# Local attention and two expert layers on one core: keys copied per lead tile, one score product per head, half the products on zeros, a fourth decode buffer

## Chip, core and metric

The kernel runs on one core of one Trainium2 chip. The metric is the device time of one execution in microseconds (us). A core has five engines that run their own instruction lists in order and wait for one another through semaphores: TensorE (PE in the profile, with its weight loads as PEld), VectorE (DVE), ScalarE (ACT), GpSimd (POOL) and SyncE (SP, which here issues the transfers).

## The reference

Inputs are q, k, v of 2 batches, 8 heads, 768 positions and 64 elements a head, and two pairs of weights. All arithmetic is float32.

```
scores_l = q @ k.T / 8           only where |pos_q - pos_k| < 16, else -1e9
scores_s = q @ max of k over blocks of 32 / 8 + log(32)
a = softmax over [scores_l, scores_s];  x = a @ [v, mean of v over blocks of 32]
x = (1536 tokens, 512);  h = relu(x @ w_in);  x = (h*h) @ w_out        2048 wide
h = x @ w_in2;  out = (h * sigmoid(h)) @ w_out2                         2048 wide
```

## The kernel before

Attention is worked out in 24 tiles of 64 queries. A tile of a batch needs 96 keys around its queries and the 24 block summaries, so 120 columns of scores (`NK`) for each head. Two heads lie side by side on the 128 partitions (a head pair, hp 0 to 3), so a head pair is two products of 64 rows that run together. The expert layers take the 1536 tokens in three blocks of 512, and each layer's 2048 hidden columns in 16 chunks of 128. A chunk s is `gemm1(s)` (tile `h`, 12 products of 512 columns), relu, square and a split into a high and a low part (`gh`, `gl`, tile `g`), then `gemm2(s)` (tile `acc`, 12 products). Every weight chunk (`wi`, `wo`) arrives as raw 64-bit numbers and is decoded: `sc` on ScalarE, `sh`, `st1`, `st2` on VectorE, `hi` on ScalarE, `lo` on VectorE. The product of `sc` lies in tile `c`, of which there are `NSPL` = 3. For `wo` chunks `c` is also written out to memory (`scr`), and the tile is free only when that transfer has landed.

The first eight tiles are the **lead**: no expert product can start before all eight are through, since the first block of 512 tokens is exactly these eight. They are loaded in bulk: `t_ksum` (all keys of batch 0, one tile for each head pair), `qrlead` (queries, two halves of four tiles), `vrows` (values for the block means), `vlead` (values, two halves). For each lead tile and head pair `psl` forms the scores on TensorE, `ttl` (line 397) adds the mask and takes the maximum on VectorE, `exl` (line 402) is the exponential on ScalarE. For each tile follow `ze`, `rc`, `nt` (the norm, VectorE), `psa` (four transposes, TensorE), `a` (a copy on ScalarE), `av` (16 short products), and `xh`, `xl` (high and low half of x, on ScalarE and VectorE). Block means of the values come from six products `vs` into tile `psv`, which ScalarE copies out in two wide copies `vmean` (24x2048 into `vlead`) ahead of the first `av`. `av` of the lead goes to one of four PSUM banks (tag `acc`), so the fifth waits for the `xl` of the first.

`psl` before takes two pairs of products for a head pair: one with 96 columns straight from a window of `t_ksum`, one with 24 columns from `ksum`. Ahead of all this TensorE runs `WARM` = 20 products on a tile of zeros (`idle_in`, `idle_out`).

The order of the first block, lead and 16 chunks with the attention of tiles 8 to 15 between them, is not written by hand: `first_order()` is a planner with a duration, a due time and dependencies for every step. It gives a fixed list, and each engine's instructions stand in the order of that list, SyncE's transfers too. After the first block a scheduler places the remaining attention tiles among the products of the second block.

Of the kernel before, what the change touches and what calls it, by code (L numbers as in the profile page):

```python
# [10 lines left out]
F32 = mybir.dt.float32  # L11
# [25 lines left out]
LAG = 2  # L37
NSPL = 3
NWO = 6
# [8 lines left out]
NGRP = 4  # L48
WARM = 20
NEG = -1.0e9  # L50
# [3 lines left out]
def first_order():  # L54
# [13 lines left out]
    def tile_due(g):  # L68
        return .25 * g if g < NLEAD else 46 + 11 * (g - NLEAD)

    def chunk_due(s):
        return 30 + 7 * s

# [5 lines left out]
    for hp in range(NHP):  # L79
        op("vec", "ksum", hp, 1.0, -50 + hp, [("kt", hp, 0)])  # L80
    for c in range(6):
        op("pe", "vs", c, .92, 1.7 + .1 * c, [("vr", c // 2, 0)])
    for i in range(NLEAD // NGRP):
# [4 lines left out]
    for j in range(4 * NHP):  # L88
        due = tile_due(TPB) - 28 + j
        load("kv", j, 196, due - 4, [("kvr", j - 2, A)] * (j >= 2))  # L90
        op("vec", "kvr", j, .52, due, [("kv", j, 0)])
# [3 lines left out]
    for g in range(NFIRST):  # L95
        due, two = tile_due(g), g - 2 >= NLEAD
        if g < NLEAD:
            for hp in range(NHP):
                op("pe", "psl", (g, hp), .38, due, [("kt", hp, 0), ("ksum", hp, A), ("q", g // NGRP, 0)] +
                   [("psl", (g, hp - 1), 0)] * (hp > 0), bank=None if hp else ("acc", "ttl", (g, NHP - 1)))  # L100
                op("vec", "ttl", (g, hp), .21, due, [("psl", (g, hp), M), ("cst", 0, 0)])
                op("act", "exl", (g, hp), .385, due, [("ttl", (g, hp), A)])
            exp = [("exl", (g, hp), A) for hp in range(NHP)]
        else:
            load("kw", g, 246, due - 9, [("pss", g - 2, M)] * two)
            load("qr", g, 131, due - 8.9, [("side", g - 2, A)] * two)
            load("vf", g, 196, due - 6, [("av", g - 2, M)] * two)
            op("pool", "side", g, 1.2, due, [("qr", g, 0)] + [("pss", g - 2, M)] * two)
            op("vec", "kwc", g, .13, due - .5, [("kw", g, 0)] + [("kvr", 4 * NHP - 1, 0)] * (g >= TPB))
            if TPB <= g < TPB + NVF:  # L110
                op("vec", "vfc", g, .35, due, [("vf", g, 0), ("vendc", 0, A)])
            op("pe", "pss", g, 1.1, due, [("kwc", g, A), ("side", g, A)] + [("gemm1", 1, 0)] * (g == NLEAD), bank=("att", "ttr", g))
            op("vec", "ttr", g, .84, due, [("pss", g, M), ("psa", g - 2, M)])
            op("act", "exp", g, 1.54, due, [("ttr", g, -.45)])
            exp = [("exp", g, A)]
# [4 lines left out]
        else:  # L120
            op("act", "nt", g, 1.2, due, [("rc", g, A)])
        op("pe", "psa", g, .62, due, [("nt", g, -.1)], bank=("att", "a", g))
        op("act", "a", g, .56, due, [("psa", g, M)] + [("av", g - 2, M)] * two)
        values = [("vl", g // NGRP, 0), ("vmean", g // NGRP, A)] if g < NLEAD else [("vf", g, 0), ("vfm", g % NVF, A)]
# [6 lines left out]
    for i, (x, s) in enumerate(chunks):  # L131
        due = chunk_due(s) - 11 + .5 * (x == "wo") - 20 * (not i)
        load("raw", (x, s), 524, chunk_due(s) - 14 + .5 * (x == "wo") - 100 * (not i),
# [23 lines left out]

    free = dict.fromkeys(("sp", "act", "vec", "pe", "pool"), 0.0)
    end, banks, moved = {}, dict(att=[], acc=[]), 2.0
# [15 lines left out]
    while todo:  # L175
# [5 lines left out]
        t, _, _, o = min(picks)  # L181
        t, _, _, o = min((p for p in picks if p[3]["eng"] == o["eng"] and p[0] <= t + .1), key=lambda p: p[1:3])
        todo.remove(o)
# [12 lines left out]
def kernel(  # L196
# [126 lines left out]
    def again_wo(kept, m, name):  # L323
# [18 lines left out]
    qd = [cp.tile([P, NHP, QT], F32, tag=f"qd{i}", name=f"qd{i}") for i in range(NQD)]  # L342
    qrlead = [first_p.tile([P, NGRP, QT * NHP], F32, tag="qr", name="qrlead0"),
              wi_p.tile([P, NGRP, QT * NHP], F32, tag="wi", name="qrlead1")]
    vlead = first_p.tile([P, NLEAD, H, D], F32, tag="vf", name="vlead")
# [95 lines left out]
    def a_copy(g):  # L441
        d = st[g]
        a = d.pop("pa")[0:NK].rearrange("p c q -> p (c q)")
        if g >= NLEAD:
            d["a"] = p2.tile([P, 512], F32, tag="a", name=f"a{g}")
        copy(act, d["a"][0:NK], a)
# [126 lines left out]
    def first_block():  # L573
# [8 lines left out]
        for _ in range(WARM):  # L582
            mm(idle_out, idle_in[:, 0:P], idle_in, start=True, stop=True)
        for g in range(NLEAD):

# [31 lines left out]


        def psl(ghp):
            g, hp = ghp  # L620
            if hp == 0:
                st[g]["ps"] = ps_acc.tile([P, NHP, NK], F32, tag="acc", name=f"pss{g}")
            q = qrlead[g // NGRP][:, g % NGRP].rearrange("p (q c) -> p c q", c=NHP)
            for keys, to in ((kts[hp][:, g * QT:g * QT + NWIN], slice(0, NWIN)), (ksum[0][:, hp], slice(NWIN, NK))):
                for e in range(2):
                    pr = slice(64 * e, 64 * e + 64)
                    mm(st[g]["ps"][pr, hp, to], q[pr, hp], keys[pr], start=True, stop=True)

# [86 lines left out]
        def xh(g):  # L715
            if g * QT >= BLOCKS[0]:
                leave_lead()
            x_high(g)

        do = dict(kt=kt, q=q, cst=cst_, vr=vr, vl=vl, ksum=ksum_, vs=vs, vmean=vmean, vfm=vfm, kv=kv, kvr=kvr,  # L720
                  vend=vend, vendc=vendc, vfc=vfc, kw=kw_load, qr=q_load, vf=v_load, side=side_by_side, kwc=k_sums,
# [174 lines left out]
```

## Time and profile before

| | us |
|---|---|
| median of 3 runs | 620.21 |
| lowest, highest | 617.1, 620.78 |
| the profiled execution, its own time | 621.01 |
| its span, first to last instruction | 619.2 |
| TensorE busy | 606.7 (98%) |
| VectorE busy | 340.3 (55%) |
| ScalarE busy | 301.3 (49%) |

The profile is of one execution. A time of 1.81 us lies around its span. Busy shares are means over stages that differ: up to about 46 us the lead runs, up to about 163 us the first block, and from there almost only products. The view by stretches tells these apart. Matmuls are pipelined, and their durations overlap, so that a busy TensorE is not one at its peak; the distance between starts says more than a product's duration.

### The profile page before, as it was taken

The page shows a single profiled execution, that of the slowest core. Times are in us where ns is not written, and L with a number is a line of the kernel's source. Part 1 is how long each engine was busy: PE and PEld are TensorE (multiplying, and loading weights), DVE is VectorE, ACT ScalarE, POOL GpSimd, SP SyncE. Part 2 cuts the span into 40 slices and gives each one's busy share as a digit, 9 for nine tenths or more (in the row PEclk, how much of TensorE's full clock was granted, in tenths as well). Part 3 has the DMA queues.
Part 4 walks back from the last instruction along what each step waited for, and adds up shares of the span by engine and source line. Part 5 has one row for each costly group of instructions (what it writes and reads, how often), then busy time and mean ns, then how long its engine had stood idle before and what let it go on. Part 6 is the DMA issues. An engine that isn't in the chain of part 4 may idle for free.

```text
span 619.2 us, 9053 instructions
## 1 busy us (share of the span) xinstructions
PE 606.7 (98%) x3332; PEld 491.2 (79%) x3332; DVE 340.3 (55%) x785; ACT 301.3 (49%) x665; POOL 52.2 (8%) x61
## 2 busy tenths in 40 slices
PE   9979999899999999999999999999999999999997
PEld 7758786677888877888888888888888888888886
DVE  4899989994455544375555687665322222322222
ACT  3779978697544544365555554443212221222221
POOL 0011000101443443100000000000000000000000
PEclk9989999999999999999999999999999999999999
DMA  9977888665355455446564334515500233400211
GB/s 302 298 209 265 260 273 279 218 208 170 133 178 198 156 178 204 153 171 214 191 202 133 105 103 169 200 73 203 169 1 2 68 103 102 137 0 1 102 35 68
DMA packets 36619, 96.51 MB, mean 156 GB/s; under 512 B 3936, under 2 KB 11232, under 8 KB 36576
## 3 DMA queue, kind: packets, MB, share of 16 engines
q1 hardware_dynamic: 36576, 95.95, 47.0%
q8 instruction: 26, 0.43, 0.3%
q14 instruction: 17, 0.14, 0.1%
HBM read 74.96 MB, written 20.97 MB: 155 GB/s over the span
## 4 chain that ended last, share of the span: by engine, by line
PE 82%; DVE 10%; DMA 4%; ACT 3%; issue 1%; DVEq 0%; ACTq 0%
PE acc L229 37%; PE h L229 37%; PE pss L229 4%; DMA t_kv<-in_kT_dram 2%; PE av L229 2%; PE idle_out L229 1%; DVE c_wo L289 1%; DMA scr_dram<-c_wo 1%; PE psa L439 1%; DVE raw_wi L285 1%; DVE c_wi L289 1%; DVE wi L237 1%; DVE raw_wo L285 1%; DVE wo L237 1%; DMA t_kv<-in_vT_dram 1%
## 5 line engine op out<-in xcount | busy, mean ns | idle before, releaser
L229 PE MATMUL h<-xt,wi 128*128 128x512 f32 x576 | 142.4, 395 | 0.0
L229 PE MATMUL acc<-g,wo 128*128 128x512 f32 x576 | 140.2, 392 | 0.2 <-DVE g L237 0.2
L229 PE MATMUL h<-xt,wj 128*128 128x512 f32 x576 | 139.0, 391 | 0.0
L229 PEld LDWEIGHTS h<-xt,wj 128*128 128x128 f32 x576 | 108.1, 188 | 23.5 <-DVE r L237 0.2
L229 PEld LDWEIGHTS acc<-g,wo 128*128 128x128 f32 x576 | 107.5, 188 | 23.5 <-issue 0.6
L229 PEld LDWEIGHTS h<-xt,wi 128*128 128x128 f32 x576 | 106.5, 188 | 23.0 <-issue 1.0
L237 DVE TENSOR_TENSOR g<-r,g 128x512 fp32r<-128x512 f32 x96 | 80.5, 838 | 74.3 <-ACT g L233 38.4
L237 DVE TENSOR_TENSOR r<-h,r 128x512 f32<-128x512 f32 x48 | 33.2, 691 | 114.2 <-ACT r L535 113.7
L535 ACT ACTIVATE r<-h 128x512 f32<-128x512 f32 x48 | 28.7, 597 | 117.5 <-PE h L229 117.4
L233 ACT ACTIVATE g<-r 128x512 fp32r<-128x512 f32 x80 | 50.5, 631 | 35.3 <-DVE r L237 34.5
L229 PE MATMUL acc<-wq,g 128*128 128x512 f32 x240 | 57.3, 390 | 0.0
L229 PE MATMUL acc<-wo,g 128*128 128x512 f32 x216 | 53.6, 397 | 0.0
L229 PEld LDWEIGHTS acc<-wq,g 128*128 128x128 f32 x240 | 45.1, 188 | 9.3
L402 ACT ACTIVATE T<-T,m 128x120 f32<-128x120 f32 x96 | 36.8, 385 | 27.5 <-DVE m L397 27.2
L229 PEld LDWEIGHTS acc<-wo,g 128*128 128x128 f32 x216 | 40.7, 188 | 9.7
L229 PE MATMUL acc<-wp,g 128*128 128x512 f32 x120 | 28.8, 390 | 0.0
L233 ACT ACTIVATE wo<-c_wo 128x512 fp32r<-128x512 f32 x38 | 23.7, 622 | 7.8 <-DVE c_wo L289 7.6
L527 ACT ACTIVATE r<-h 128x512 f32<-128x512 f32 x16 | 9.6, 598 | 34.6 <-PE h L229 34.6
L229 PEld LDWEIGHTS acc<-wp,g 128*128 128x128 f32 x120 | 22.5, 188 | 4.7
L234 POOL COPY qd<-qr 128x256 f32<-128x256 f32 x16 | 14.9, 930 | 133.3 <-PE pss L229 85.3
L397 DVE CUSTOM_DVE_ANT_0 T<-pss,cst_sb 128x120 f32<-128x120 f32 x96 | 21.9, 276 | 7.3 <-PE pss L229 7.3
L237 DVE TENSOR_TENSOR wj<-c_wj,wj 128x512 fp32r<-128x512 f32 x16 | 11.1, 691 | 23.4 <-ACT wj L233 23.4
(78 smaller groups left out, 603.3 us busy)
## 6 DMA issues: line engine op xcount, KB each, us to landing
raw_wo<-in_w_out_dram SPq DMA_DIRECT2D x22, 512.0 KB, 4.3
wq<-split SPq DMA_DIRECT2D x20, 512.0 KB, 3.3
raw_wi<-in_w_in_dram SPq DMA_DIRECT2D x16, 512.0 KB, 5.0
split<-wo SPq DMA_DIRECT2D x16, 512.0 KB, 3.3
raw_wj<-in_w_in_dram SPq DMA_DIRECT2D x16, 512.0 KB, 3.6
wo<-split SPq DMA_DIRECT2D x16, 512.0 KB, 3.3
raw_wp<-in_w_out_dram SPq DMA_DIRECT2D x10, 512.0 KB, 3.5
split<-wp SPq DMA_DIRECT2D x10, 512.0 KB, 3.1
```

Of the source, the lines that this page charges most:

```text
L229: pe.matmul(o, l, r, **kw)
L233: return act.activation(out=o, in_=i, func=AF.Copy, scale=scale)
L234: return eng.tensor_copy(out=o, in_=i)
L237: return eng.tensor_tensor(out=o, in0=a, in1=b, op=op)
L285: vec.scalar_tensor_tensor(out=low, in0=high, scalar=SIGN, in1=low, op0=ALU.bitwise_and, op1=ALU.bitwise_or)
L289: vec.scalar_tensor_tensor(out=c, in0=c, scalar=3, in1=raws.pop(name)[:, :, 0], op0=ALU.logical_shift_left, op1=ALU.bitwise_or)
L397: vec.tensor_tensor_reduce(out=d["T"][:, c], in0=d["ps"][:, c], in1=cst_sb[:, kind * NK:kind * NK + NK], scale=-0.125, scalar=3.0e38, op0= ...
L402: act.activation(out=d["T"][:, c], in_=d["T"][:, c], func=AF.Exp, bias=d["m"][:, c:c + 1], scale=-1.0, accum_out=d["z"][:, c:c + 1])
L439: pe.transpose(ps[0:NK, c], d["T"][:, c], id_sb)
L527: act.activation(out=r, in_=h, func=AF.Relu)
L535: act.activation(out=r, in_=h, func=AF.Sigmoid)
```

## The change

Keys of the lead are copied. For each half of the lead (four tiles) and each pair of head pairs there is now a tile `kws` of 4 times 120 columns: ScalarE copies the four windows of 96 keys in one instruction (`kwl`, 128x4x96), VectorE copies the 24 summaries four times in one (`ksl`, 128x4x24), 8 instructions each. `psl` then takes one pair of products of 120 columns for a head pair in place of two pairs. `WARM` falls from 20 to 10. `NSPL` rises from 3 to 4. The first half of the queries moves to another pool of the same size, and the copy tile `a` of the later tiles has one buffer in place of two, so that a tile's `a` now waits for the `av` of the tile before. In the planner due times move (chunks by 6 us earlier, the decode of a chunk by no change in all, transposes by 2 us), a picked step must be ready at once (`t + .1` becomes `t`), and TensorE is taken as busy up to 5.6 us.

```diff
-NSPL = 3
+NSPL = 4
-WARM = 20
+WARM = 10
     def chunk_due(s):
-        return 30 + 7 * s
+        return 24 + 7 * s
     for hp in range(NHP):
         op("vec", "ksum", hp, 1.0, -50 + hp, [("kt", hp, 0)])
+        for i in range(NLEAD // NGRP):
+            op("act", "kwl", (hp, i), .5, -50 + hp + 51 * i, [("kt", hp, 0)])
+            op("vec", "ksl", (hp, i), .13, -50 + hp + 48 * i, [("ksum", hp, 0)])
     for c in range(6):
-        op("pe", "vs", c, .92, 1.7 + .1 * c, [("vr", c // 2, 0)])
+        op("pe", "vs", c, .92, 2.7 + .1 * c, [("vr", c // 2, 0)])
...
-        due = tile_due(TPB) - 28 + j
+        due = tile_due(TPB) - 20 + j
...
-                op("pe", "psl", (g, hp), .38, due, [("kt", hp, 0), ("ksum", hp, A), ("q", g // NGRP, 0)] +
+                op("pe", "psl", (g, hp), .29, due, [("kwl", (hp, g // NGRP), A), ("ksl", (hp, g // NGRP), A), ("q", g // NGRP, 0)] +
...
-        op("pe", "psa", g, .62, due, [("nt", g, -.1)], bank=("att", "a", g))
-        op("act", "a", g, .56, due, [("psa", g, M)] + [("av", g - 2, M)] * two)
+        op("pe", "psa", g, .62, due - 2, [("nt", g, -.1)], bank=("att", "a", g))
+        op("act", "a", g, .56, due, [("psa", g, M)] + [("av", g - 1, M)] * (g > NLEAD))
...
-        due = chunk_due(s) - 11 + .5 * (x == "wo") - 20 * (not i)
+        due = chunk_due(s) - 5 + .5 * (x == "wo") - 20 * (not i)
...
-    free = dict.fromkeys(("sp", "act", "vec", "pe", "pool"), 0.0)
+    free = dict(sp=0.0, act=0.0, vec=0.0, pe=5.6, pool=0.0)
...
-        t, _, _, o = min((p for p in picks if p[3]["eng"] == o["eng"] and p[0] <= t + .1), key=lambda p: p[1:3])
+        t, _, _, o = min((p for p in picks if p[3]["eng"] == o["eng"] and p[0] <= t), key=lambda p: p[1:3])
...
-            d["a"] = p2.tile([P, 512], F32, tag="a", name=f"a{g}")
+            d["a"] = p2.tile([P, 512], F32, tag="a", bufs=1, name=f"a{g}")
...
+        def kwl(hpi):
+            hp, i = hpi
+            w = kts[hp][:, i * NGRP * QT:i * NGRP * QT + NWIN]
+            copy(act, kws[i][hp // 2][:, hp % 2, :, 0:NWIN], bass.AP(w.tensor, w.offset, [w.ap[0], [QT, NGRP], w.ap[1]]))
+
+        def ksl(hpi):
+            hp, i = hpi
+            s = ksum[0][:, hp]
+            copy(vec, kws[i][hp // 2][:, hp % 2, :, NWIN:NK], bass.AP(s.tensor, s.offset, [s.ap[0], [0, NGRP], s.ap[1]]))
...
-            for keys, to in ((kts[hp][:, g * QT:g * QT + NWIN], slice(0, NWIN)), (ksum[0][:, hp], slice(NWIN, NK))):
-                for e in range(2):
-                    pr = slice(64 * e, 64 * e + 64)
-                    mm(st[g]["ps"][pr, hp, to], q[pr, hp], keys[pr], start=True, stop=True)
+            for e in range(2):
+                pr = slice(64 * e, 64 * e + 64)
+                mm(st[g]["ps"][pr, hp], q[pr, hp], kws[g // NGRP][hp // 2][pr, hp % 2, g % NGRP], start=True, stop=True)
```

How the lists of instructions change is shown at three places. TensorE at its start, before:

```order
L229 MATMUL idle_out<-idle_in 128x512 x20
L229 MATMUL pss_211<-t_ksum_0_180,qrlead_103 64x96 x2
L229 MATMUL pss_211<-ksum_201,qrlead_103 64x24 x2
L229 MATMUL pss_218<-t_ksum_0_180,qrlead_103 64x96 x2
L229 MATMUL pss_218<-ksum_201,qrlead_103 64x24 x2
```

and TensorE at its start with the change (`kws` are the copied keys):

```order
L232 MATMUL idle_out<-idle_in 128x512 x10
L232 MATMUL pss_209<-kws_0_130,qrlead_103 64x120 x2
L232 MATMUL pss_212<-kws_0_130,qrlead_103 64x120 x2
L232 MATMUL pss_217<-kws_0_130,qrlead_103 64x120 x2
L232 MATMUL pss_222<-kws_0_130,qrlead_103 64x120 x2
```

Half of the zero products are gone, and each tile and head pair has one row where it had two.

ScalarE from the last exponentials of the lead to its last high half, before (`vlead` are the two wide copies, `xt` the high halves, `c` and `wi`, `wo` the decode):

```order
L402 ACTIVATE T_175,z_178<-T_175,m_177 128x120 x2
L233 ACTIVATE c_wo_527<-raw_wo_207 128x512
L233 ACTIVATE a_171<-psa_520 120x512
L233 ACTIVATE c_wi_538<-raw_wi_209 128x512
L233 ACTIVATE vlead<-psv_118 24x2048 x2
L233 ACTIVATE xt_85<-av_556 128x4x64
L233 ACTIVATE xt_85<-av_569 128x4x64
L233 ACTIVATE xt_85<-av_580 128x4x64
L233 ACTIVATE a_176<-psa_542 120x512
L233 ACTIVATE xt_85<-av_591 128x4x64
L233 ACTIVATE xt_85<-av_606 128x4x64
L233 ACTIVATE wo_631<-c_wo_527 128x512
```

and ScalarE at the same place with the change:

```order
L404 ACTIVATE T_169,z_172<-T_169,m_171 128x120 x3
L236 ACTIVATE a_160<-psa_453 120x512
L404 ACTIVATE T_169,z_172<-T_169,m_171 128x120
L236 ACTIVATE vlead<-psv_118 24x2048 x2
L236 ACTIVATE xt_85<-av_492 128x4x64
L236 ACTIVATE xt_85<-av_503 128x4x64
L236 ACTIVATE xt_85<-av_512 128x4x64
L236 ACTIVATE a_165<-psa_470 120x512
L236 ACTIVATE xt_85<-av_523 128x4x64
L236 ACTIVATE a_170<-psa_485 120x512
L236 ACTIVATE xt_85<-av_537 128x4x64
L236 ACTIVATE xt_85<-av_550 128x4x64
```

Of the two decode steps that stood ahead of the wide copies, one now stands behind the sixth high half and one (not shown) behind the eighth; and the last two copies `a` stand behind the wide copies, where only one did.

VectorE around the low halves of the lead, before:

```order
L237 TENSOR_TENSOR xt_85<-av_606,xt_85 128x4x64
L651 TENSOR_REDUCE ksum_644<-t_kv_265 128x12
L237 TENSOR_TENSOR xt_85<-av_619,xt_85 128x4x64
L237 TENSOR_TENSOR wo_631<-c_wo_527,wo_631 128x512
L237 TENSOR_TENSOR xt_85<-av_633,xt_85 128x4x64
L237 TENSOR_TENSOR xt_85<-av_647,xt_85 128x4x64
```

and with the change:

```order
L240 TENSOR_TENSOR xt_85<-av_537,xt_85 128x4x64
L240 TENSOR_TENSOR xt_85<-av_550,xt_85 128x4x64
L237 COPY kw_233<-ksum_195 128x4x24
L292 SCALAR_TENSOR_TENSOR c_wo_584<-c_wo_584,raw_wo_205 128x512
L240 TENSOR_TENSOR xt_85<-av_561,xt_85 128x4x64
L240 TENSOR_TENSOR xt_85<-av_575,xt_85 128x4x64
```

Up to the last low half VectorE has one join of `c`, one low part of `wo` and one reduction of later keys less ahead of it than before, and eight copies `ksl` more. Among SyncE's transfers the raw numbers of the first `wi` now stand ahead of the second half of `vlead`. From the first `gemm1` to the end TensorE changes 38 times from expert products to attention products, before 34 times.

## Rows read from the trace of the kernel before

**Rows 1.** The page's first line, the whole span.

```profile
span 619.2 us, 9053 instructions
```

**Rows 2.** Chain of waits by time: start us, us, engine, tile, line, count.

```profile
1.45 7.63 PE idle_out L229 x20
...
9.08 9.23 PE pss L229 x152
...
41.55 3.66 PE av L229 x64
```

**Rows 3.** Stretches: busy (count) of PE, PEld, DVE, ACT, POOL; granted clock; DMA share; GB/s.

```profile
9.00:35.60 26.60, 26.44 (x301) 20.23 (x300) 21.71 (x121) 19.61 (x76) 0.65 (x1) 1.00 1.02 298
35.60:41.50 5.90, 2.12 (x65) 1.95 (x64) 5.59 (x11) 4.83 (x7) 0.99 (x1) 1.00 0.76 234
41.60:44.90 3.30, 3.30 (x62) 3.30 (x64) 2.89 (x9) 2.09 (x5) 0.00 (x0) 0.50 0.53 202
46.00:131.00 85.00, 82.45 (x513) 64.40 (x509) 80.83 (x198) 71.80 (x174) 5.97 (x6) 1.00 0.77 255
```

**Rows 4.** The same view of the products on zeros alone.

```profile
1.40:7.10 5.70, 5.65 (x13) 4.52 (x14) 1.00 0.91 286
```

**Rows 5.** Groups, 9 to 46 us: count | busy us, mean ns | idle before.

```profile
L229 PE MATMUL pss<-t_ksum,qrlead 64*64 64x96 f32 x128 | 14.9, 309 | 0.0
...
L229 PE MATMUL pss<-ksum,qrlead 64*64 64x24 f32 x128 | 11.2, 247 | 0.0
...
L229 PE MATMUL pss<-kw,qd 64*64 64x120 f32 x16 | 1.0, 269 | 0.0
...
L229 PE MATMUL psv<-vrows,share 128*24 128x512 f32 x12 | 5.7, 597 | 0.0
...
L439 PE MATMUL psa<-cst_sb,T 128*120 128x128 f32 x32 | 5.4, 289 | 0.2 <-DVE T L433 0.2
...
L229 PE MATMUL av<-a,vlead 120*64 120x64 f32 x128 | 5.7, 269 | 3.8 <-DVE xt L237 2.5 <-ACT vlead L233 1.4
...
L233 ACT ACTIVATE a<-psa 120x512 f32<-120x512 f32 x8 | 4.7, 593 | 2.6 <-PE psa L439 2.4
...
L233 ACT ACTIVATE xt<-av 128x256 fp32r<-128x256 f32 x8 | 2.9, 388 | 2.7 <-PE av L229 2.7
...
L234 DVE COPY kw<-ksum 128x96 f32<-128x96 f32 x2 | 0.3, 198 | 0.0
```

**Rows 6.** VectorE by time: start us, us, instruction [idle before, releaser].

```profile
8.09 0.95 DVE L615 TENSOR_REDUCE ksum<-t_ksum 128x24 f32<-128x768 f32 x1 [3.40 <-DMA t_ksum<-in_kT_dram]
...
9.71 0.28 DVE L397 CUSTOM_DVE_ANT_0 T<-pss,cst_sb 128x120 f32<-128x120 f32 x1 [0.67 <-PE pss L229]
```

**Rows 7.** Transfers issued up to 9 us: count, KB each, us to landing.

```profile
vlead<-in_vP_dram SPq DMA_DIRECT2D x2, 768.0 KB, 14.9
...
cst_sb<-in_cst_dram SPq DMA_DIRECT2D x1, 244.0 KB, 6.5
```

**Rows 8.** Waits from 9.5 to 46 us: total us, times, longest.

```profile
ACT T L402 <- DVE m L397: 10.6, 5, 8.0
...
DVE T L397 <- PE pss L229: 3.5, 10, 1.2
...
ACT xt L233 <- PE av L229: 2.7, 2, 2.3
...
ACT a L233 <- PE psa L439: 2.4, 4, 1.1
```

**Rows 9.** Waits from 36 to 140 us, same columns.

```profile
ACT c_wi L233 <- DMA scr_dram<-c_wo: 3.4, 1, 3.4
...
PE psa L439 <- ACT T L431: 2.6, 3, 1.4
```

**Rows 10.** TensorE by time, the first three chunks of the expert layer.

```profile
46.08 8.45 PE L229 MATMUL h<-xt,wi 128*128 128x512 f32 x36
```

**Rows 11.** The page's groups: one VectorE step over 128x512.

```profile
L237 DVE TENSOR_TENSOR wj<-c_wj,wj 128x512 fp32r<-128x512 f32 x16 | 11.1, 691 | 23.4 <-ACT wj L233 23.4
```

More of the change, by code (lines that the diff above doesn't have):

```diff
@@ L68, in tile_due @@
     def tile_due(g):
-        return .25 * g if g < NLEAD else 46 + 11 * (g - NLEAD)
+        return 0.25 * g if g < NLEAD else 46 + 11 * (g - NLEAD)
     def chunk_due(s):
-        return 30 + 7 * s
+        return 24 + 7 * s
     for i, (name, arg, kb) in enumerate([("kt", 0, 393), ("q", 0, 524), ("kt", 1, 393), ("cst", 0, 250), ("kt", 2, 393),
@@ L342 @@
     qd = [cp.tile([P, NHP, QT], F32, tag=f"qd{i}", name=f"qd{i}") for i in range(NQD)]
-    qrlead = [first_p.tile([P, NGRP, QT * NHP], F32, tag="qr", name="qrlead0"),
-              wi_p.tile([P, NGRP, QT * NHP], F32, tag="wi", name="qrlead1")]
+    qrlead = [wi_p.tile([P, NGRP, QT * NHP], F32, tag="wi", name=f"qrlead{i}") for i in range(NLEAD // NGRP)]
     vlead = first_p.tile([P, NLEAD, H, D], F32, tag="vf", name="vlead")
@@ L583, in first_block @@
             mm(idle_out, idle_in[:, 0:P], idle_in, start=True, stop=True)
+        kws = [[wi_p.tile([P, 2, NGRP, NK], F32, tag="wi", name=f"kws{i}_{j}") for j in range(NHP // 2)]
+               for i in range(NLEAD // NGRP)]
         for g in range(NLEAD):
@@ L718, in xh @@
             x_high(g)
-        do = dict(kt=kt, q=q, cst=cst_, vr=vr, vl=vl, ksum=ksum_, vs=vs, vmean=vmean, vfm=vfm, kv=kv, kvr=kvr,
+        do = dict(kt=kt, q=q, cst=cst_, vr=vr, vl=vl, ksum=ksum_, kwl=kwl, ksl=ksl, vs=vs, vmean=vmean, vfm=vfm, kv=kv, kvr=kvr,
                   vend=vend, vendc=vendc, vfc=vfc, kw=kw_load, qr=q_load, vf=v_load, side=side_by_side, kwc=k_sums,
```

## The prediction

> **What bounds the kernel now.** I read the span first: 619.2 us [rows 1], in a profiled execution of 621.01 us, so 1.8 us lie around it. That execution is 0.8 us above the median of 620.21; I make the sum against 621.0 and take 0.8 off at the end. Then I read the chain of waits in order of time: the reader is to see that TensorE carries it without a break from 1.45 us, first with products on zeros, then with 152 score records in 9.23 us [rows 2]. The view by stretches says the same: TensorE is busy 26.44 of 26.60 us up to 35.6, VectorE 21.71 and ScalarE 19.61 [rows 3]. From 35.6 to 41.5 it works 2.12 of 5.90 us, and right behind that the granted clock is 0.50, the lower of its two levels, 1.2 GHz [rows 3]. The first expert product starts at 46.08 [rows 10]. From 46 to 131 all three are nearly full: TensorE 82.45 of 85 us, VectorE 80.83, ScalarE 71.80 [rows 3]. Behind that the profile is almost products alone. So whatever the change is worth must come from the start of the first expert product, now 46.08, and from the waits between there and 131.
>
> **Zero products.** Thirteen of the twenty begin in 5.7 us [rows 4], 0.44 us apart, while expert products of the same 512 columns are 8.45 / 36 = 0.23 apart [rows 10]. (The 1.00 beside them can't be their clock; that record seems to begin later.) Ten fewer take 4.4 us off TensorE. That alone gains little: the mask lands at 2.2 + 6.5 = 8.7 us [rows 7], and the second maximum of keys starts at 8.09, when its transfer has landed [rows 6]; with its 0.95 us and two small copies VectorE is free for the first `ttl` at about 9.2. It starts at 9.71 now [rows 6], so 0.5 us.
>
> **Scores.** 152 records are 19 head pairs of 8, 0.49 us each [rows 2]. A product of 120 columns is in the trace already, for later tiles: four head pairs in 1.0 us, 0.25 each [rows 5]. So 32 x 0.24 = 7.7 us leave TensorE. That the joined product costs as much as the two is thereby excluded.
>
> **Copies of keys.** A ScalarE copy of 256 elements takes 388 ns, one of 512 takes 593 [rows 5]; 384 elements lie between, and I take 0.48 as the middle. Eight are 3.8 us. Four come before the first exponential, where ScalarE idles 8.0 us [rows 8]; four, 1.9 us, stand among the exponentials. If that cover goes it is 3.8. `ksl` has the size of a copy that takes 198 ns [rows 5]: 8 x 0.2, of which four ahead of 9.2 and 0.8 us behind.
>
> **The lead as a whole.** TensorE's lead before the last `av` falls to 7.9 for scores, 5.4 for transposes and 5.7 for block means [rows 5], 19 us from 9.2 on, so it is not what is late next; VectorE is, with ScalarE close behind. VectorE: 0.5 us earlier; one join, one low part and one reduction less ahead of the last low half (about 0.69, 0.69 [rows 11] and 0.5), -1.9; `ksl` +0.8; and it waits 3.5 us for scores [rows 8], of which at least half should go, as scores are now made twice as fast. That is 3.3 to 5.1 us. To it comes the slow `av`: 64 records take 3.66 us at the low clock [rows 2], out of 5.7 for 128 [rows 5], so the other 64 took 2.0; 1.6 us more if TensorE no longer waits so long in front of them. It should not, since the low halves stand ready earlier (the decode that sat ahead of them in ScalarE's list is gone). Together 3.3 to 6.7. ScalarE has to follow: +1.9 for copies, three steps of 0.59 less [rows 5], and waits of 2.6 (10.6 less the first 8.0), 2.4 and 2.7 us [rows 8] that may end earlier. A new wait stands in its list: the decode of the first `wi` comes some exponentials earlier than its raw numbers may have landed. They land no later than the second half of `vlead` does now, which is issued before 9 us and takes 14.9, so about 24 us [rows 7]; nothing but the attention of three tiles is queued behind. I allow for 0 to 1.5. I take **-6.2** for the lead, near the upper end, because TensorE has 7 us of air there, and keep -3.3 to -8.
>
> **Decode.** With three buffers `c`, ScalarE once waits 3.4 us until a `scr` transfer has landed [rows 9], and the norms queued behind it are what TensorE waits for: 2.6 us in all from 36 to 140, three times, 1.4 the longest [rows 9]. With four buffers that one should go. That is as much as TensorE stands idle from 46 to 131 at all (85 less 82.45 [rows 3]); I take **-1.5**, bounds -2.6 and +1.5, since a list in another order may make a wait of its own.
>
> **What costs nothing or little.** Four more changes between expert and attention products: none to one product of 0.23 us each [rows 10], I take **+0.5**. The second half of `vlead` behind 512 KB of raw numbers: about 2 us later, and not read before 31. One buffer for `a`: the `av` it waits for stands ahead of its transposes on TensorE, and only ScalarE's `xh` and decode are queued behind it; without that cover about one copy, 0.6. The moved queries: nothing.
>
> Sum: 621.0 - 6.2 - 1.5 + 0.5 = 613.8, less 0.8: **613.0**.
>
> **A rule that speaks against it.** Right behind 5.9 us with 2.12 of work the granted clock is at its lower level, and from 46 us on, after full work, it is 1.00 again [rows 3]. With 19 us of work where there were 26 TensorE will have more gaps in the lead. The Trainium skill, page "TensorE: Matmul & The Clock Gate", section "The HAM clock gate", says that the array is throttled by default and that activity releases it; by that rule alone ten zero products fewer, and gaps where scores stood back to back, leave the lead at the lower level, and the sum would be the 624 of the last rival below. The trace agrees as far as its one fall shows; no run here has the lead with such gaps.
>
> **Rivals.**
>
> *It is given back.* VectorE is 95% busy from 46 to 131 and loses only 4.2 us there [rows 3]. If the earlier expert products run into it (a `gl` or `lo` late for the next product, a transfer late for a decode), half of the lead's gain returns as waits: 621.0 - 3.5 - 0.8 = about 617. For: the shares. Against: VectorE's list up to the first `gl` is as long as before, so it too comes earlier. 20%.
>
> *ScalarE takes TensorE's place in the lead*: copies and the early decode cost what the scores save: within 2 us, 619. For: 19.6 of 26.6 us busy [rows 3]. Against: 7.7 us of its waits were for others. 8%.
>
> *All waits go*: lead -8, every wait behind it -2.6, less the 0.8: about 610. 15%.
>
> *The clock stays low in the lead.* The price: `av` at the low level takes 3.66 / 2.0 = 1.8 times as long. 19 us of TensorE become 34, from 9.2 to 43, where it stood at 35.6. It decides once more than half of the work is at the low level (19 x 1.4 = 26.6). With 80% it is 31 us, 4.6 late; less 1.0 for waits: 621.0 + 3.6 - 0.8 = about 624. For: more gaps. Against: at the low level the same work leaves fewer gaps, and the one fall in the trace was over by 46 us [rows 3]. 7%.
>
> That leaves 50% for the forecast, whose own range is 610 to 616.5 from the bounds of its terms.
>
> **Numbers.** 613.0. The range of 8 in 10 takes in most of the first rival and of the fast case: 609.0 to 618.5. A measurement of this kernel tells about 1% from no change, that is 614.0 and 626.4. Of the forecast's 50% about 60% lie below 614, with all of the fast case and a little of the first rival: faster 0.47. Slower 0.05: most of the clock case, whose 624 is close to that bound and passes it if all of the lead is at the low level. The same 0.48.
>
> **What would show it.** The first expert product at about 40 us and not 46; score records 0.25 us per head pair; the first `ttl` at 9.2; no wait of VectorE for scores above 0.3 us; a granted clock of 1.00 where the last `av` runs; no ScalarE wait for `scr`; TensorE's waits from there to the end of the first block under 2 us. I am wrong if the first expert product is as early as that and TensorE waits more behind it, or if the granted clock is 0.50 for much of 10 to 35 us, or if ScalarE's wait for the first raw numbers is over 2 us.

## The result, and the profile after

The changed kernel takes 612.6 us, median of 4 runs, beside 619.5 us for the kernel before on the same chip: ratio 0.9897, 95% interval 0.9861 to 0.9934, so 1.0% faster and just past what a measurement of this kernel can tell. The forecast was 613.0. The profiled execution of the changed kernel has a span of 612.3 us where [rows 1] has 619.2. A later set of runs gave 613.74 beside 620.57, ratio 0.9897 again, and a second profiled execution with a span of 610.4.

TensorE by time, changed kernel, first execution (start us, us, instruction, what it waited for ahead of it):

```profile
5.67 1.22 PE L232 MATMUL pss<-kws,qrlead 64*64 64x120 f32 x16 [0.23 <-ACT kws L236]
9.46 1.59 PE L232 MATMUL pss<-kws,qrlead 64*64 64x120 f32 x16 [2.57 <-DVE m L399]
11.75 4.99 PE L232 MATMUL pss<-kws,qrlead 64*64 64x120 f32 x60 [0.70 <-DVE kws L237]
...
30.95 0.81 PE L441 MATMUL psa<-cst_sb,T 128*120 128x128 f32 x4 [1.49 <-DVE T L435]
31.68 5.50 PE L232 MATMUL av<-a,vlead 120*64 120x64 f32 x128
37.47 1.04 PE L232 MATMUL pss<-kw,qd 64*64 64x120 f32 x16 [0.28 <-issue]
38.43 8.55 PE L232 MATMUL h<-xt,wi 128*128 128x512 f32 x36
```

The first expert product starts at 38.43 us, 7.65 earlier than in [rows 10]. The first scores come in short groups with waits between them; in [rows 2] they were one unbroken run. The view by stretches, same columns as [rows 3]:

```profile
9.00:35.60 26.60, 23.68 (x236) 16.81 (x238) 24.29 (x134) 24.07 (x84) 0.65 (x1) 0.87 1.05 293
11.50:14.70 3.20, 2.95 (x30) 2.98 (x32) 2.63 (x16) 2.30 (x9) 0.00 (x0) 0.50 1.07 382
31.90:35.20 3.30, 3.30 (x68) 3.30 (x66) 2.62 (x7) 2.53 (x5) 0.47 (x1) 0.50 1.00 248
46.00:131.00 85.00, 81.67 (x507) 63.44 (x506) 81.93 (x207) 72.45 (x181) 5.11 (x6) 1.00 0.83 269
```

From 9 to 35.6 us VectorE is now busy 24.29 us (21.71 in [rows 3]) and ScalarE 24.07 (19.61): they have taken the lead over from TensorE, which fell from 26.44 to 23.68. Two stretches have the granted clock at 0.50, the lower of its two levels, each behind a wait of TensorE (2.57 and 0.70 us ahead of the first, 1.49 ahead of the second). Behind 46 us little has changed: TensorE misses 3.33 of 85 us (2.55 in [rows 3]). The groups, as in [rows 5], and the waits, as in [rows 8] and [rows 9]:

```profile
L236 ACT ACTIVATE kws<-t_ksum 128x384 f32<-128x384 f32 x4 | 1.9, 508 | 0.0
```

```profile
PE psa L441 <- DVE T L435: 1.5, 1, 1.5
ACT T L404 <- DVE m L399: 1.4, 2, 0.8
...
DVE T L399 <- PE pss L232: 0.7, 2, 0.4
```

```profile
ACT c_wo L236 <- DMA scr_dram<-c_wo: 2.2, 2, 2.0
```

One copy of keys takes 508 ns. VectorE's 3.5 us of waiting for scores are 0.7. ScalarE's 10.6 us of waiting for VectorE are 1.4, but 8.0 of the 10.6 were one wait ahead of the first exponential; in its place ScalarE now waits 3.8 and 1.8 us for keys to land, between its copies, and 0.6 for VectorE. Behind the first exponential 2.6 us became 0.8. The wait for a `scr` transfer is still there, 2.0 us in one piece where [rows 9] has 3.4.

### The profile page after: what moved, and what is told of

Its sections match the earlier page's. It is cut to its first block, busy times and chain, and to the rows that moved or that the text cites. A ratio compares the mean times of both kernels' runs of the same rounds, so it can differ in the third digit from the quotient of the medians.

```text
span 612.3 us, 8782 instructions
## 1 busy us (share of the span) xinstructions
PE 598.4 (98%) x3194; PEld 481.6 (79%) x3194; DVE 338.2 (55%) x793; ACT 304.4 (50%) x673; POOL 50.5 (8%) x61
## 4 chain that ended last, share of the span: by engine, by line
PE 82%; DVE 11%; DMA 5%; issue 1%; ACT 1%; SPq 0%; DVEq 0%
PE acc L232 39%; PE h L232 39%; DMA raw_wi<-in_w_in_dram 3%; PE pss L232 2%; PE av L232 2%; DMA t_kv<-in_kT_dram 1%; DVE wi L240 1%; DVE c_wo L292 1%; PE psa L441 1%; DVE wo L240 1%; DVE raw_wo L288 1%; DMA cst_sb<-in_cst_dram 1%; DVE c_wi L292 1%; DVE raw_wi L288 1%; DVE g L240 1%
## 5 line engine op out<-in xcount | busy, mean ns | idle before, releaser
L240 DVE TENSOR_TENSOR g<-r,g 128x512 fp32r<-128x512 f32 x96 | 78.6, 818 | 72.7 <-ACT g L236 37.3
L237 POOL COPY qd<-qr 128x256 f32<-128x256 f32 x16 | 12.9, 808 | 136.6 <-PE pss L232 62.0
```

The costliest lines, as they stand in the source:

```text
L237: return eng.tensor_copy(out=o, in_=i)
L240: return eng.tensor_tensor(out=o, in0=a, in1=b, op=op)
```

## The experiments

Two questions. **What made the lead shorter:** scores at half the price (theory L), the new order of the lists (theory O), or TensorE's clock (theory C)? **What holds TensorE up behind the lead:** a full VectorE (theory G1), or single steps that stand too late in their lists (theory G2)? All ran beside the kernel before on the same chip. The table takes apart one profiled execution of each. "First" is the start of the first expert product, "idle" is TensorE's time without work from there to 140 us, read from the view by stretches, and "rest" is the span less both.

| kernel | median us | ratio to before, 95% | first | idle | rest |
|---|---|---|---|---|---|
| before | 619.4 to 620.6 | 1 | 46.1 | 3.4 | 569.7 |
| changed, first profile | 612.60 | 0.9897 (0.9861 to 0.9934) | 38.4 | 3.3 | 570.5 |
| changed, again | 613.74 | 0.9897 (0.9870 to 0.9925) | 36.2 | 3.9 | 570.3 |
| old planner numbers | 620.78 | 1.0015 (0.9996 to 1.0034) | 41.6 | 4.6 | 572.6 |
| new planner numbers alone | 625.28 | 1.0092 (1.0068 to 1.0116) | 47.9 | 3.7 | 571.5 |
| scores as two products | 618.28 | 0.9991 (0.9973 to 1.0010) | 41.5 | 4.3 | 570.1 |
| twenty zero products | 612.88 | 0.9900 (0.9876 to 0.9925) | 36.7 | 2.9 | 570.2 |
| fillers in the lead | 613.63 | 0.9900 (0.9871 to 0.9929) | 40.2 | 4.2 | 570.4 |
| three buffers c | 612.56 | 0.9881 (0.9853 to 0.9910) | 36.9 | 4.3 | 569.6 |
| fewer reductions | 611.62 | 0.9850 (0.9822 to 0.9879) | 37.7 | 1.9 | 569.6 |
| kwc early | 615.85 | 0.9922 (0.9896 to 0.9948) | 37.4 | 3.9 | 573.2 |
| 12 low halves on GpSimd | 622.25 | 1.0031 (1.0011 to 1.0051) | 37.4 | 9.1 | 574.4 |
| 6 low halves on GpSimd | 617.70 | 0.9965 (0.9944 to 0.9987) | 37.8 | 6.1 | 574.3 |
| copies of keys on GpSimd | 614.87 | 0.9921 (0.9895 to 0.9946) | 39.3 | 4.1 | 572.5 |

The rest is 569.6 to 570.5 us wherever the granted clock is 1.00 from the first expert product to 140 us, but for the new numbers alone with 571.5. It is 572.5 to 574.4 in the five kernels where the clock is 0.97 or 0.98 there. So nearly all differences are in the first column, in the second, and in where a stretch at the low clock falls.

The two profiled executions of the changed kernel differ by 2.3 us in the first column; the second was expected within 0.5 us of the first. It was the fastest of its six executions, the first was the slowest of its four, so the usual place probably lies between. Some 0.9 of the 2.3 us come from the transfer of keys. VectorE's second reduction of keys waits for it and starts so in the first execution and in the second:

```profile
7.80 0.95 DVE L619 TENSOR_REDUCE ksum<-t_ksum 128x24 f32<-128x768 f32 x1 [2.73 <-DMA t_ksum<-in_kT_dram]
```

```profile
6.86 0.95 DVE L619 TENSOR_REDUCE ksum<-t_ksum 128x24 f32<-128x768 f32 x1 [1.76 <-DMA t_ksum<-in_kT_dram]
```

Another 1 us is the low clock over the last `av`, shown below. A difference of 1 us or less in the first column therefore tells nothing about a kernel.

With scores as two products, twenty zero products, fillers and fewer reductions, the lists are those of the changed kernel, but for the products added. In the other variants the planner makes a new list, so more than the named step moves.

### Old planner numbers under the new products

```diff
-        return 24 + 7 * s
+        return 30 + 7 * s
...
-        due = chunk_due(s) - 5 + .5 * (x == "wo") - 20 * (not i)
+        due = chunk_due(s) - 11 + .5 * (x == "wo") - 20 * (not i)
```

and so for the other numbers of the planner.

> The changed kernel with the planner's old numbers (due times, TensorE free from 0, the pick within 0.1): copied keys, one product per head, ten zero products and four buffers stay. The changed kernel's own first expert product starts at 38.4 us, that of the kernel before at 46.1. Theory L (the lead is shorter since a score costs half and TensorE no longer holds VectorE up): the first expert product stays early, at 40 us or before (at most 41), and the time is 613 to 615. Theory O (it is the new order of the lists, with the decode moved out of ScalarE's way): the first expert product goes back to 44 to 46 us and the time to 618 or more.

The whole gain is gone, 620.78 us. The first expert product is neither early nor late, 41.62, so neither theory had it right alone. TensorE by time:

```profile
31.20 5.15 PE L232 MATMUL av<-a,vlead 120*64 120x64 f32 x112 [1.42 <-ACT vlead L236]
38.26 1.07 PE L441 MATMUL psa<-cst_sb,T 128*120 128x128 f32 x4 [1.91 <-DVE T L435]
40.01 1.12 PE L232 MATMUL av<-a,vlead 120*64 120x64 f32 x16 [0.69 <-ACT a L236]
41.62 10.34 PE L232 MATMUL h<-xt,wi 128*128 128x512 f32 x36 [0.48 <-ACT xt L236]
```

With the decode due early again, the last tile's norms come late: its transposes wait 1.91 us at 38.26, and its `av` is done 3.9 us later than in the changed kernel. Behind these waits comes a stretch at the low clock, now over expert products: the first 36 take 10.34 us where they take 8.55. With the old numbers the products, copies and buffers are worth 4.5 us in the first column, and the later waits (4.6 against 3.4) and the low clock under expert products take it back. The list is not that of the kernel before either: ahead of the lead's last low half VectorE has five joins of `c` and two low parts of weights, where the kernel before has three and two and the changed kernel two and one.

### New planner numbers alone

```diff
-        return 30 + 7 * s
+        return 24 + 7 * s
```

and the other numbers, in the kernel before.

> The kernel before with the planner's new numbers alone: two products per head and key kind, twenty zero products, three buffers. Theory L: the first expert product at 45 to 47.5 us, time 618 to 621, nothing gained. Theory O: the first expert product at 40 to 42 us and a time of 613 to 615.

Slower by 0.9%: theory O is refuted as a cause by itself, and L's figure (nothing gained) was too kind. TensorE by time and by stretch:

```profile
17.89 0.55 PE L229 MATMUL pss<-t_ksum,qrlead 64*64 64x96 f32 x4 [0.40 <-DVE m L397]
...
21.30 1.11 PE L439 MATMUL psa<-cst_sb,T 128*120 128x128 f32 x4
```

```profile
20.00:24.00 4.00, 4.00 (x29) 3.22 (x28) 2.60 (x19) 1.19 (x2) 0.00 (x0) 0.50 1.07 227
```

TensorE is nearly full here (24.62 of 26.6 us from 9 to 35.6), but behind two waits of 0.40 us the granted clock is 0.50 from about 18 to 25 us, and four transposes take 1.11 us where they take 0.66 at full clock in the changed kernel. A second such stretch runs from 28.4 to 35.2, and the mean from 9 to 35.6 is 0.74. It is no accident of one profile: all six executions have a mean granted clock of 0.986 to 0.989, those of the kernel before beside them 0.995 to 1.000. VectorE waits 7.7 us for scores from 9 to 36, so TensorE bounds the lead and does it more slowly. What the order alone would be worth at the full clock, no run shows. A low clock in the lead is what the fourth rival of the prediction priced; it came here, in a kernel that was not forecast and whose scores are not halved.

### Scores as two products of copied keys

```diff
-            for e in range(2):
-                pr = slice(64 * e, 64 * e + 64)
-                mm(st[g]["ps"][pr, hp], q[pr, hp], kws[g // NGRP][hp // 2][pr, hp % 2, g % NGRP], start=True, stop=True)
+            for to in (slice(0, NWIN), slice(NWIN, NK)):
+                for e in range(2):
+                    pr = slice(64 * e, 64 * e + 64)
+                    mm(st[g]["ps"][pr, hp, to], q[pr, hp], kws[g // NGRP][hp // 2][pr, hp % 2, g % NGRP, to], start=True, stop=True)
```

> The changed kernel, with the same lists, but each head's score again as two products, of 96 and of 24 columns, both from the copied keys. TensorE gets the 7.7 us back that the change took off it. Theory L: TensorE is the bound of the lead again, VectorE waits for scores by 2 us or more, the first expert product moves from 38.4 to 43 to 46 us and the time from 612.6 to 617 to 620. Theory O: the first expert product stays within 1 us of 38.4.

```profile
9.36 9.63 PE L232 MATMUL pss<-kws,qrlead 64*64 64x96 f32 x152 [1.19 <-DVE m L399]
...
34.82 0.81 PE L441 MATMUL psa<-cst_sb,T 128*120 128x128 f32 x4 [1.50 <-DVE T L435]
35.56 2.08 PE L232 MATMUL av<-a,vlead 120*64 120x64 f32 x64
...
41.49 8.48 PE L232 MATMUL h<-xt,wi 128*128 128x512 f32 x36
```

The lists are word for word those of the changed kernel, so this is the price of the products alone: the first expert product 3.1 us later than in the first profile (5.3 later than in the second), the time 618.28, and the gain gone. VectorE waits 3.9 us for scores from 9 to 36 us, 0.7 in the changed kernel. Theory L holds for the time and for this wait; the place was expected a little later (43 to 46).

### The clock: twenty zero products, and fillers in the gaps

```diff
-WARM = 10
+WARM = 20
```

> The changed kernel with twenty zero products in place of ten. In the changed kernel the granted clock is 0.50 at 11.4 to 14.8 us, right behind a stretch with gaps. If the ten products fewer let the clock fall (theory C), this stretch at 0.50 goes, and what TensorE gets back, half of 3.4 us, shows in a first expert product up to 1 us earlier. By theory L TensorE has air in the lead, so the clock there costs nothing: the first expert product is at 38.4 to 39.5 us, later by what the first ttl is late (9.0 to 9.4), and the time within 1.5 us of 612.6 whether the 0.50 stays or goes.

In its profile the stretches at 0.50 are gone from the lead, and `av` runs at full speed:

```profile
30.50 2.08 PE L232 MATMUL av<-a,vlead 120*64 120x64 f32 x64
33.06 2.38 PE L232 MATMUL av<-a,vlead 120*64 120x64 f32 x64 [0.47 <-DVE xt L240]
...
36.72 8.46 PE L232 MATMUL h<-xt,wi 128*128 128x512 f32 x36
```

Four of its six executions have a mean granted clock of 1.000, where none of the ten of the changed kernel is above 0.997. The time is the same, 0.9900 against 0.9897. The second execution of the changed kernel says why one profile misleads here. It has the early stretch at 0.50 and ten zero products, and yet its `av` ran at full speed:

```profile
30.35 2.08 PE L232 MATMUL av<-a,vlead 120*64 120x64 f32 x64
32.61 2.37 PE L232 MATMUL av<-a,vlead 120*64 120x64 f32 x64 [0.18 <-DVE xt L240]
35.19 1.04 PE L232 MATMUL pss<-kw,qd 64*64 64x120 f32 x16 [0.20 <-issue]
36.15 8.55 PE L232 MATMUL h<-xt,wi 128*128 128x512 f32 x36
```

So the early stretch costs nothing that is seen at the end: from the reduction that waits for the keys to the last norm of the lead it is 22.9 us in this execution and 22.9 with twenty zero products. The late one is in one of the two profiled executions, for about 1 us of `av`.

```diff
+            filled[0] += 1
+            if filled[0] == 9:
+                for _ in range(8):
+                    mm(idle_out, idle_in[:, 0:P], idle_in, start=True, stop=True)
...
+            if g == NLEAD - 1:
+                for _ in range(5):
+                    mm(idle_out, idle_in[:, 0:P], idle_in, start=True, stop=True)
```

> The changed kernel with the same lists and 13 more products on zeros where TensorE waits in the lead: eight behind the first 16 score records (a wait of 2.6 us) and five ahead of the last transposes (a wait of 1.5 us). In the run with twenty zero products the granted clock was 1.00 all through the lead, the 128 av records took 4.5 us in place of 5.5 and the first expert product came at 36.7. Theory C (TensorE's gaps in the lead make the 0.50 stretches, and the one over av costs): no stretch at 0.50 between 10 and 36 us, av in 4.2 to 4.6 us, first expert product at 36.7 to 37.7, time 1 to 1.5 us less. Rival (what ends the lead is VectorE and ScalarE, not the clock): first expert product within 0.4 us of 38.4 and no change of the time.

```profile
9.49 1.94 PE L232 MATMUL pss<-kws,qrlead 64*64 64x120 f32 x16 [2.46 <-DVE m L399]
11.36 3.78 PE L232 MATMUL idle_out<-idle_in 128*128 128x512 f32 x8
```

No gain, 613.63, and for the clock inconclusive: the eight fillers stand behind the second group of scores, not the first, so the wait of 2.46 us stayed. They began at the low clock, took 3.78 us and pushed the lead back. The five late ones did fill their wait, and `av` ran in 4.5 us, without effect on the time. Two of the six executions have a mean granted clock of 1.000; they took 612.1 and 616.2 us.

### Behind the lead: three buffers, fewer reductions, an earlier copy

```diff
-NSPL = 4
+NSPL = 3
```

> The changed kernel with three buffers c for the decode in place of four (the planner, which knows the number, orders the lists anew). If the fourth buffer is worth what the forecast took for it, the time rises by about 1.5 us (bounds 0 to 2.6) and ScalarE waits for a scr transfer by 3 us or more. Theory that it is worth nothing (in the changed kernel ScalarE still waits 2.0 us for scr, and TensorE still waits 3.3 us from 36 to 140): time within 0.7 us, waits of TensorE from 36 to 140 between 2.8 and 4.2 us.

Nothing: 0.9881 against 0.9897. The fourth buffer is worth nothing here; TensorE's idle time is 4.3 us with three and 3.3 to 3.9 with four, near what two executions differ by and without a trace in the time. ScalarE, for which a wait of 3 us was expected, does not wait for `scr` at all there from 36 to 140 us.

```diff
-            vec.tensor_reduce(out=sums[:, hp, i * n:(i + 1) * n], in_=halves.pop(j).rearrange("p (n j) -> p n j", j=KBLK),
+            vec.tensor_reduce(out=sums[:, hp, i * n:(i + 1) * n], in_=halves.pop(j).rearrange("p (n j) -> p n j", j=KBLK)[:, :, 0:KBLK // 4],
```

> The changed kernel with the second batch's block maxima and means (16 reductions at 44 to 115 us) over a quarter of each block: three quarters of that batch's keys and values are left out of them. The lists stay as they are; VectorE has some 5 us less to do there. TensorE waits 3.3 us from 36 to 140. Theory G1 (VectorE is too full, 95%, so single steps come late): TensorE waits 1.5 us less or better, time 1.5 to 3 us less. Theory G2 (single steps stand too late in lists that run in order): the waits stay above 2.5 us and the time within 0.7 us.

611.62 us beside 613.74 for the changed kernel on the same chip. TensorE's waits from 36 to 140 us with the lighter VectorE, and in the second execution of the changed kernel:

```profile
PE pss L232 <- DMA scr_dram<-c_wo: 1.4, 1, 1.4
PE av L232 <- ACT a L236: 0.4, 1, 0.4
PE pss L232 <- issue: 0.3, 1, 0.3
```

```profile
PE pss L232 <- DVE kw L237: 1.4, 1, 1.4
PE av L232 <- ACT a L236: 1.3, 2, 0.8
PE psa L441 <- ACT T L433: 1.2, 1, 1.2
```

The norm's wait, at 81 us, goes, and so does the longer of the two for `a`, at 99; TensorE idles 2.0 us less, and the median falls by 2.1, though the 95% intervals of the two ratios just overlap. The 16 reductions, which start at 71 to 103 us, took 4.8 us less in all. For the waits among them that is G1. The wait for the small copy, at 109, is not touched: in both kernels TensorE waits 1.45 us there and goes on 0.26 us behind VectorE's copy `kw`, though the profile names another releaser in the first.

```diff
-            op("vec", "kwc", g, .13, due - .5, [("kw", g, 0)] + [("kvr", 4 * NHP - 1, 0)] * (g >= TPB))
+            op("vec", "kwc", g, .13, due - 5, [("kw", g, 0)] + [("kvr", 4 * NHP - 1, 0)] * (g >= TPB))
```

> The changed kernel with the small copy of block maxima ahead of each later tile's scores due 5 us before them in place of 0.5. In the changed kernel TensorE waits 1.6 us at 111 us for one such copy, which stands behind a minimum and an expert step in VectorE's list. Theory G2: this wait goes (below 0.3 us), waits from 36 to 140 are 2 us or less, and the time is 0.8 to 1.6 us less. Theory G1: the wait is taken over by another, waits stay at 3 us or more, time within 0.7 us.

```profile
PE av L232 <- ACT a L236: 2.7, 3, 1.3
PE pss L232 <- issue: 0.7, 1, 0.7
PE psa L441 <- ACT T L433: 0.6, 1, 0.6
```

```profile
120.00:140.00 20.00, 20.00 (x129) 15.08 (x128) 14.39 (x35) 15.13 (x35) 0.80 (x2) 0.91 0.51 153
```

The wait for the copy is gone and `av` waits in its place, for as much in all (3.9 us idle in both). The kernel is slower than the changed one, 615.85: behind a wait of 1.34 us that ends at 118 comes a stretch at the low clock over expert products, from 120 to 123.5. G2's gain did not come; the wait moved.

### GpSimd for VectorE's work

```diff
-        op("vec", "lo", (x, s), .61, due, [("hi", (x, s), A)])
+        on_pool = x == "wo" and 1 <= s <= 12
+        op("pool" if on_pool else "vec", "lo", (x, s), 1.28 if on_pool else .61, due, [("hi", (x, s), A)])
...
-            sub(vec, ws[xs][:, 1], cs[xs].bitcast(F32), ws[xs][:, 0].bitcast(F32))
+            x, s = xs
+            sub(pool if x == "wo" and 1 <= s <= 12 else vec, ws[xs][:, 1], cs[xs].bitcast(F32), ws[xs][:, 0].bitcast(F32))
```

and the same with `s in (1, 3, 5, 7, 9, 11)` in the second.

> The changed kernel with the low halves of twelve wo chunks (1 to 12 of the first block) subtracted on GpSimd in place of VectorE; the planner knows it. VectorE loses 12 x 0.78 = 9.4 us of work, most of it between 46 and 131, where it is 96% busy; GpSimd, 5 us busy there, gets 12 x 1.28 = 15.4 us. Theory G1 (a full VectorE makes TensorE's waits behind the lead): VectorE is under 90% busy from 46 to 131, TensorE waits 1 to 2 us less than 3.3 to 3.9, and the time falls by 1 to 2.5 us. Theory G2 (it is where single steps stand in the lists): the waits only move, time within 1 us or, where the GpSimd step is late for its product, up to 2 us longer.

> The same for six wo chunks only (1, 3, 5, 7, 9, 11): VectorE loses 4.7 us, as much as in the run with fewer reductions, which took 2.1 us off the time. Theory G1: time 1 to 2 us less than the changed kernel's, TensorE waits from 36 to 140 about 2 to 2.8 us. Theory G2: within 1 us.

Slower than the changed kernel in both, by about 1.3% and 0.7% of the time. VectorE did not get lighter. GpSimd and VectorE by time, with twelve moved:

```profile
44.10 1.81 POOL L241 TENSOR_TENSOR wo<-c_wo,wo 128x512 fp32r<-128x512 f32 x1
```

```profile
44.67 1.79 DVE L293 SCALAR_TENSOR_TENSOR c_wo<-c_wo,raw_wo 128x512 int32<-128x512 int32 x1
...
46.83 0.70 DVE L289 SCALAR_TENSOR_TENSOR raw_wo<-raw_wo 128x512 int32<-128x512 int32 x1
```

The VectorE step that meets GpSimd's subtraction ends 0.55 us after it, after 1.79 us where such a step takes 0.70 alone. Eleven of the twelve subtractions meet a step so and add 11.2 us to VectorE's work, more than the 12 times 0.69 that were taken off it. From 46 to 131 VectorE is busy 82.5 us with twelve moved and 81.9 with none. The decode comes later, TensorE idles 9.1 us, and the low clock follows. The Trainium skill, page "SBUF — State Buffer", section "Who interferes with whom", says that VectorE and GpSimd share one pair of ports under an exclusive lock, that a VectorE instruction with two inputs in SBUF contends with a GpSimd instruction that reads there, and that the order of issue decides which of the two is blocked. The trace agrees: GpSimd's subtraction began first, at 44.10, and 1.1 us were added to the VectorE step begun at 44.67. The test of G1 that these two were meant to be is void, since VectorE's load didn't fall.

```diff
-            op("act", "kwl", (hp, i), .5, -50 + hp + 51 * i, [("kt", hp, 0)])
+            op("pool" if i else "act", "kwl", (hp, i), 1. if i else .5, -50 + hp + 51 * i, [("kt", hp, 0)])
...
-            copy(act, kws[i][hp // 2][:, hp % 2, :, 0:NWIN], bass.AP(w.tensor, w.offset, [w.ap[0], [QT, NGRP], w.ap[1]]))
+            copy(pool if i else act, kws[i][hp // 2][:, hp % 2, :, 0:NWIN], bass.AP(w.tensor, w.offset, [w.ap[0], [QT, NGRP], w.ap[1]]))
```

> The changed kernel with the second group's four copies of keys (4 x 0.51 us, which stand among ScalarE's exponentials) made by GpSimd, which has nothing else to do up to 35 us. In the changed kernel VectorE and ScalarE are busy 24.3 and 24.1 of 26.6 us in the lead and TensorE 23.7. Theory S (ScalarE's copies are on the path of the lead now): the first expert product 1 to 2 us earlier than 36.2 to 38.4, time 1 to 2 us less. Theory V (VectorE is as much the bound, and the fourth group of exponentials follows it): first expert product within 0.7 us of that, time within 1 us of the changed kernel's. If GpSimd's copies hold VectorE's steps up as its subtractions did (1.79 us beside one, 0.69 alone), the lead is 1 to 4 us longer.

614.87 us, ratio 0.9921 where the changed kernel has 0.9897, and the first expert product at 39.25. So taking 2 us of copies off ScalarE gains nothing, and the 1 to 2 us of theory S did not come. VectorE is busy 25.3 of the 26.6 us here, and TensorE's last `av` waits for its low halves:

```profile
34.75 3.50 PE L232 MATMUL av<-a,vlead 120*64 120x64 f32 x64 [1.96 <-DVE xt L240]
```

That speaks for V, but the run does not test S alone. Its new list has one join and one low part more on VectorE ahead of the lead's last low half. From the keys to the last norm it is 22.3 us here and 22.9 in the second execution of the changed kernel, so the copies may be worth 0.6 us that this list loses again. The time is 1.1 us above the changed kernel's, a little more than V allowed; two stretches at the low clock over later products, at 86 and 117 us, go with it. A GpSimd copy took 0.50 to 0.51 us, and VectorE's steps beside one (a reduction in 0.95 us, minima in 0.28) were as long as elsewhere.

## Why the prediction was right, and where it was not

The time was met, 613.0 for 612.6, with two terms off in opposite directions: the gain of the lead was sized too small, and the one from the waits behind it should have been nothing. So the mechanism of the lead was right, and that the time was met so closely is in part luck.

**Zero products, scores, copies.** Ten zero products fewer bring the first scores from 9.08 to 5.67 us, 3.4 earlier, where I took 4.4 off; nothing came of the difference, since VectorE waits for keys until 7.80. The first `ttl` starts at 9.03 (forecast 9.2), and at 8.10 in the second profile, where the keys land earlier. Fifteen head pairs of scores take the 4.99 us of the third row above, 0.24 each at full clock and 0.40 in the low stretch (forecast 0.25). The copies are 508 ns (forecast 480). The new wait of ScalarE for the first raw numbers is 0.2 us (allowed 0 to 1.5).

**The lead, -6.2: measured -7.65 in the first profile and -9.9 in the second.** Two terms were small. The order of the lists I counted as one join, one low part and one reduction less, -1.9. Against the first profile, the run with the old numbers puts the order at 3.2 us before the first expert product, and at 1.3 us of waits and 1.8 us of low clock behind it; but its list has two joins more than the kernel before, so part of that is the list's own. The halved scores I took as "at least half" of 3.5 us of waits; the run with two products puts them at 3.1 against the first profile. The two are no plain sum: the new order without the halved scores is a loss of 1.8 us in the first column and 5.7 in the time, with TensorE still the bound and half of the lead at the low clock. None of the parts that were run alone gives the 1%. The bounds of my terms add up to about 610 to 619 and not to 616.5.

**The clock.** Wrong for the first profile: I forecast 1.00 where the last `av` runs, and half of its 128 records ran at 0.50, 5.50 us in all, so the 1.6 us of the slow `av` weren't regained there. The second profile has 4.6 us. With gaps in the lead the granted clock is 0.87 from 9 to 35.6 us, and 0.94 in the second profile, 1.00 before. The rule of the Trainium skill weighed in the prediction (page "TensorE: Matmul & The Clock Gate", section "The HAM clock gate": throttled by default, released by activity) thus pointed at something real. It decided nothing: the scores have slack at either level, and twenty zero products, with the clock at 1.000 in four executions of six, don't change the time.

**Waits behind the lead, -1.5: measured about 0.** TensorE idles 3.4 us before, 3.3 and 3.9 after. I put its waits down to ScalarE's wait for `scr`. That wait shrank and TensorE's didn't, and with three buffers it was gone and the time the same. What showed in its place: norms and `a` come late while VectorE is full, and 4.8 us less for it took 2.0 us off these waits and 2.1 off the time. The small copy stands late in its list; moved forward by a new list, it handed its wait to `av`.

**Four more changes of kind, +0.5.** The rest of the span grew from 569.7 to 570.3 and 570.5. That is of the size taken; no run measured it by itself.

**The rivals.** "Given back" (617) is refuted as a net effect: what stands behind the first expert product is 573.1 us before and 573.9 and 574.3 after, so about 1 us of 8 to 10 was given back. ScalarE alone did not take TensorE's place; VectorE and ScalarE did together, at 24.3 and 24.1 of 26.6 us. The low clock for much of the lead came only in the kernel that has the order without the products.

**Still open.** What sets off the late stretch at 0.50. It is not the length of the wait of 1.49 us ahead of it alone: the kernel with scores as two products waits 1.50 us at that place and its `av` runs at the full clock, as in the second profile behind 1.04. The one buffer for `a` and the single numbers of the planner were not run by themselves.

## What to carry to other kernels

Work taken off the engine that bounds a stretch, and an order of the lists made for its new length, can be worth something only together, as here, where each alone gave nothing or a loss; measure them apart before crediting either. Where VectorE was 95% busy, less work for it shortened the waits, and moving one late step did not. GpSimd was no place for subtractions with two inputs beside a VectorE so full. Take a second profile before explaining 2 us of a first one.

## What the hardware showed that was not expected

- A VectorE step of 0.69 us took 1.79 us beside a GpSimd subtraction over 128x512. GpSimd's strided copies of keys (0.50 us) held nothing up, but beside them stood reductions with one input and minima of scores in PSUM. GpSimd's copies of queries (128x256) do hold VectorE up in the changed kernel: six of its two-input steps over 128x512 took 1.11 to 1.15 us there in place of 0.69, and each ended 0.55 us after GpSimd's copy.
- A score product of 64 rows and 120 columns pays for the low clock with 0.40 for 0.24 us per head pair, four transposes with 1.11 for 0.66.
